# Attention beside a gated feed-forward: queries in bursts of eight heads, values three heads behind the scores, output projection one head later

## The chip, the cores and the metric

The kernel runs on one core of one Trainium2 chip. The metric is the device time of one execution in microseconds (us): the median of three runs before is 560.81 (560.77 to 560.82).

Engine names as the profile has them: PE is TensorE (matmul), PEld its weight loads, DVE is VectorE, ACT is ScalarE, POOL is GpSimd, SP is SyncE. "SPq" or "POOLq" is an engine's queue of instructions, where DMAs are issued. PSUM has eight banks of 512 float32 columns.

## What is computed

The input x has 2048 rows of 448. It is layer-normalized and goes two ways: through attention with 16 query heads of 256 over the last 512 keys and values of a cache (8 key-value heads, each for two query heads), and through a feed-forward of width 1792. The result is x plus the product of both.

```
xn = layernorm(x)
q = xn @ wq                      # 16 heads of 256
p = softmax(q @ k.T / 16)        # the last 512 keys of each of 8 groups
s = (p @ v) @ wo
g = silu((gelu(xn @ w_gate) * (xn @ w_up)) @ w_down)
out = x + s * g
```

## The kernel before

The rows are cut into four chunks of 512 (`NQC`), each chunk into four tiles of 128 (`TPC`). Every operation is recorded with what it reads and writes (`Rec.op`, lines 65 to 96); the order of recording is the order on each engine, and a wait is put in where an operation depends on one of another engine. Each engine works its own list in that order.

**First part (lines 506 to 521).** For each chunk: gate and up projection with two 64-row matmuls side by side (L370), gelu (L374), product (L376), down projection (L382). The down projection of the last chunk is kept back to fill gaps at the start of attention (`fill`, lines 527 to 530).

**Second part (lines 531 to 559), attention.** There are 64 steps i, one for each chunk and head (`NI` = 4 x 16). Within a step, t runs over the four row tiles:

- `scores(i, t)`: two matmuls (L420) into bank 4 or 5 in turn; ScalarE's exponential with row sum (L424) into a buffer `pr`; VectorE's reciprocal (L426) and normalization (L427); a DMA transpose on SP's queue into `pT` (L236). Nine buffers `pr` are used in turn.
- `values(i', e_)`: at t = 0 and 2, four matmuls (L440) for half of an earlier head, and a copy into `oT` (L446 on VectorE, L448 on ScalarE for the last two heads). It is called for the first time at step 10 of scores (4i + t >= 10), so it runs two and a half heads behind. Its bank follows a list of eight that repeats every four heads: `(0, 6, 0, 6, 0, 1, 6, 6)`; at heads with i%4 = 3 both calls use bank 6.
- `outproj(G, t, part)`: at t = 1 and 3, from head 6 on, four matmuls each (L460). One head's two calls finish one row tile t of a group G of four heads; group G takes heads 4G + 6 to 4G + 9. The sum over groups is kept in `acc` by VectorE (L479, L481). After the last group of a chunk (G = 3, 7, 11; in the last chunk after G = 14) GpSimd multiplies by the gate into `tmp[t % 2]` (L485) and adds x (L487), into `ofin` or, in the last chunk, `acc`. When all four tiles are done, POOL's queue sends `ofin` out and loads the next chunk's `xr` (L233).
- `q_burst(G)`: after the first scores and values of heads with i%4 = 3, the queries of the next four heads: 56 matmuls of 64 rows (L406), which run side by side in pairs, into banks 0 to 3, and four evictions by ScalarE (L410), each for two heads, into `qT` (six heads).
- `silu(n)`: after heads 7, 10, 13, ... 52. ScalarE's tanh of half the gate into `tmp[n % 2]` (L499), and two GpSimd operations (L500, L502).

**The end (lines 549 to 559).** After the last scores, five calls of values and two of outproj are left ("vvovovv"), then group 15, in pieces and with the final operations on VectorE (L469, L471) and the output DMAs.

`tmp` is one buffer with two slots. It is used by `silu` and by the finishing of a chunk.

Of the kernel before, what the change touches and what calls it, by code (L numbers as in the profile page):

```python
# [5 lines left out]
ACT = mybir.ActivationFunctionType  # L6
ALU = mybir.AluOpType
BF16 = mybir.dt.bfloat16
# [3 lines left out]
P = 128  # L12
# [129 lines left out]
def bass_recurrent_scan__sliding_block_cached__geglu_ffn__prompt_kernel(nc, A_x, A_k, A_v, A_wq, A_wo, B_x, B_wg, B_wu, B_wd, out):  # L142
    _, S, D = A_x.shape
    Hkv, Sk, Dh = A_k.shape[1], A_k.shape[2], A_k.shape[3]
    HD = A_wq.shape[1]
    Hq = HD // Dh
# [12 lines left out]
    with es:  # L159
        off = [16512]  # L160

        def sb(name, shape, dt, at=None):
            n = 4 if dt == F32 else 2
            for x in shape[1:]:
                n *= x
            if at is None:
                at = off[0]
                off[0] += (n + 31) // 32 * 32
            return R.place(name, shape, dt, at), at + (n + 31) // 32 * 32
# [24 lines left out]
        hb, ffn_end = sb("hb", [P, NHB, QC], BF16)  # L194


        NPT = 4
        qT, at = sb("qT", [P, 6, NE, QC], BF16, gu_at)
        oT = [None, None]
        oT[0], at = sb("oT0", [P, 4 * NE, QC], BF16, at)  # L200
        xr, at = sb("xr", [P, TPC, D], BF16, at)
        assert at <= x_at
        pT, at = sb("pT", [P, NPT, NJ, QC], BF16, x_at)
        pr = []
        while at + 2 * W <= d_at:
            t_, at = sb("pr%d" % len(pr), [P, W], BF16, at)
            pr.append(t_)
        at = hb_at
        while at + 2 * W <= ffn_end:
            t_, at = sb("pr%d" % len(pr), [P, W], BF16, at)  # L210
            pr.append(t_)
        NPR = len(pr)
        oT[1], at = sb("oT1", [P, 4 * NE, QC], BF16, d_at)
        acc, at = sb("acc", [P, TPC, D], F32, at)
        tmp, at = sb("tmp", [P, 2, D], F32, at)
        ofin, at = sb("ofin", [P, TPC, D], BF16, at)
        assert at <= hb_at, (at, hb_at)
        psum = es.enter_context(nc.psum_tensor("ps", [P, 8 * 512], F32))

        def bank(b, n=512):  # L220
            return psum[:, b * 512:b * 512 + n]
# [171 lines left out]
        NI = NQC * Hq  # L393
        NG = NI // 4

        def q_burst(G):

            c, h0 = divmod(4 * G, Hq)
            for n in range(4):
                hp, e_ = divmod(n, 2)  # L400
                s, i = 2 * (n % 2) if G else (4, 0, 2, 0)[n], (4 * G + 2 * hp) % 6

                def run(e, hp=hp, e_=e_, s=s):
                    for k in range(NK):
                        for b, lo in ((s, 0), (s + 1, HP)):
                            ins = e.matmul(bank(b), lhsT=wq[lo:lo + HP, k, h0 // 2 + hp, e_ * P:(e_ + 1) * P],  # L406
                                           rhs=xnT[lo:lo + HP, c, k, :], start=k == 0, stop=k == NK - 1)
                    return ins
                pe(run, r=xn(c) + [("wq", lo, k) for lo in range(2) for k in range(NK)], w=[("ps", s), ("ps", s + 1)])
                act(lambda e, e_=e_, s=s, i=i: e.activation(  # L410
                    qT[:, i:i + 2, e_, :], psum[:, s * 512:(s + 2) * 512].rearrange("p (a q) -> p a q", a=2), ACT.Copy),
                    r=[("ps", s), ("ps", s + 1)], w=[("qT", i, e_), ("qT", i + 1, e_)])

        def scores(i, t):
            g, n = (i % Hq) // 2, i * TPC + t
            b, s = 4 + n % 2, n % NPR

            def run(e):
                for k in range(NE):
                    ins = e.matmul(bank(b), lhsT=qT[:, i % 6, k, t * P:(t + 1) * P], rhs=kT[:, g, k, :],  # L420
                                   start=k == 0, stop=k == NE - 1)
                return ins
            pe(run, r=[("kT", g), ("qT", i % 6, 0), ("qT", i % 6, 1)], w=[("ps", b)])
            act(lambda e: e.activation(pr[s][:, :], bank(b), ACT.Exp, scale=scale, accum_out=den[:, s:s + 1]),  # L424
                r=[("ps", b)], w=[("pr%d" % s,), ("den", s)])
            dve(lambda e: e.reciprocal(rden[:, s:s + 1], den[:, s:s + 1]), r=[("den", s)], w=[("rden", s)])  # L426
            dve(lambda e: e.tensor_scalar(pr[s][:, :], pr[s][:, :], rden[:, s:s + 1], None, op0=ALU.mult),  # L427
                r=[("pr%d" % s,), ("rden", s)], w=[("pr%d" % s,)])
            dmaT(pT[:, i % NPT, :, t * P:(t + 1) * P], pr[s][:, :], r=[("pr%d" % s,)], w=[("pT", i % NPT, t)], lane="p%d" % s)

        def values(i, e_):
            g = (i % Hq) // 2
            idx = (i % 4) * NE + e_
            at = 2 * i + e_ + 5

            b = (0, 6, 0, 6, 0, 1, 6, 6)[at % 8] if at < 2 * NI else (0, 6, 0, 6, 1)[at - 2 * NI]

            def run(e):
                for j in range(NJ):
                    ins = e.matmul(bank(b), lhsT=V[:, j, g, e_ * P:(e_ + 1) * P], rhs=pT[:, i % NPT, j, :],  # L440
                                   start=j == 0, stop=j == NJ - 1)
                return ins
            pe(run, r=[("pT", i % NPT, t) for t in range(TPC)] + [("V", j) for j in range(NJ)], w=[("ps", b)])
            dst, key = oT[(i // 4) % 2][:, idx, :], ("oT%d" % ((i // 4) % 2), idx)
            if i < NI - 2:
                dve(lambda e: e.tensor_copy(dst, bank(b)), r=[("ps", b)], w=[key])  # L446
            else:
                act(lambda e: e.activation(dst, bank(b), ACT.Copy), r=[("ps", b)], w=[key])  # L448

        def outproj(G, t, part, half=None):  # L450

            n8 = 4 * NE
            lo, hi = (0, D) if half is None else (half * D // 2, (half + 1) * D // 2)
            b = ((2, 2), (3, 5), (7, 4), (0, 6))[t][half or 0] if G == NG - 1 else (7, 7, 7, 4)[t] if G == NG - 2 else 7
            c, h0 = divmod(4 * G, Hq)
            end = c == NQC - 1

# [10 lines left out]
            if end and h0 == Hq - 4:  # L468
                dve(lambda e: e.tensor_tensor(tmp[:, t % 2, lo:hi], bank(b, D)[:, lo:hi], gy[:, n, lo:hi], ALU.mult),  # L469
                    r=[("ps", b), ("gy", n)], w=[("tmp", t % 2)])  # L470
                dve(lambda e: e.tensor_tensor(ofin[:, t, lo:hi], tmp[:, t % 2, lo:hi], acc[:, t, lo:hi], ALU.add),  # L471
                    r=[("tmp", t % 2), ("acc", t)], w=[("ofin", t, lo)])
                if t == TPC - 1:
                    dma("sync" if half else "scalar", o_view[:, c, t, lo:hi], ofin[:, t, lo:hi], r=[("ofin", t, lo)])
                elif half != 0:
                    dma("sync", o_view[:, c, t, :], ofin[:, t, :], r=[("ofin", t, 0), ("ofin", t, lo)])
                return
            if h0 == 0:
                dve(lambda e: e.tensor_copy(acc[:, t, :], bank(b, D)), r=[("ps", b)], w=[("acc", t)])  # L479
# [1 line left out]
                dve(lambda e: e.tensor_tensor(acc[:, t, :], bank(b, D), acc[:, t, :], ALU.add),  # L481
                    r=[("ps", b), ("acc", t)], w=[("acc", t)])
            if h0 == Hq - 4 or end and h0 == Hq - 8:
                dst, key = (acc, ("acc", t)) if end else (ofin, ("ofin", t))
                pool(lambda e: e.tensor_tensor(tmp[:, t % 2, :], acc[:, t, :], gy[:, n, :], ALU.mult),  # L485
                     r=[("acc", t), ("gy", n)], w=[("tmp", t % 2)])
                pool(lambda e: e.tensor_tensor(dst[:, t, :], tmp[:, t % 2, :], xr[:, t, :], ALU.add),  # L487
                     r=[("tmp", t % 2), ("xr",)], w=[key])
                if t == TPC - 1 and not end:
                    dma("gpsimd", o_view[:, c, :, :], ofin[:, :, :], r=[("ofin", t) for t in range(TPC)])  # L490
                    load_xr(c + 1)

        def load_xr(c):
            dma("gpsimd", xr[:, :, :], x_view[:, c, :, :], w=[("xr",)])

        def silu(n):

# [23 lines left out]
                    load_piece()  # L521
        assert not pieces
        act(lambda e: e.activation(small[:, 2:3], small[:, 0:1], ACT.Exp), r=[("eps",)], w=[("warm",)])
        q_burst(0)
        load_xr(0)

        fill = {}
# [5 lines left out]
        for i in range(NI):  # L533
            for t in range(TPC):
                scores(i, t)
                if 4 * i + t in fill:
                    down(NQC - 1, *fill[4 * i + t])
                if t % 2 == 0 and 4 * i + t >= 10:
                    values(*pv.pop(0))
                if 6 <= i and t % 2:  # L540
                    outproj(*outs[0], range(2 * t - 2, 2 * t + 2))
                    if t == TPC - 1:
                        outs.pop(0)
                if t == 0 and i % 4 == 3 and i + 1 < NI:
                    q_burst(i // 4 + 1)
            if 7 <= i and (i - 7) % 3 == 0 and (i - 7) // 3 < NT:
                silu((i - 7) // 3)

        for what in "vvovovv":
            if what == "v":  # L550
                values(*pv.pop(0))
            else:
                outproj(*outs.pop(0), range(4 * NE))
# [36 lines left out]
```

## Time and profile before

| what | value |
|---|---|
| median of 3 runs | 560.81 us |
| the profiled execution, whole | 561.18 us |
| its span from first to last instruction | 559.4 us |
| granted TensorE clock | 1.000 |
| VectorE normalization L427, one | 416 ns mean |
| exponential L424, one | 597 ns |
| eviction of a query pair L410, one | 1024 ns |
| transposes of the probabilities, issue to landing | 2.4 us median, 256 of them |

The profile is taken from one execution, whose own time is 0.37 us above the median of the others. Durations come from it. The busy time of TensorE is the sum of stretches in which at least one matmul runs; matmuls are pipelined, so one lasts 379 ns although the next starts much sooner. In the timeline a row gives start, length, engine, line, operation and tiles; "x4" merges four like operations, and a bracket tells how long the engine stood idle before it and who released it.

### The profile page before, as it was taken

Reading aid. Unit: us, or ns where it says so; the run is one execution under the profiler, and the core shown is the slowest. Engines: PE = TensorE matmul, PEld = TensorE weight load, DVE = VectorE, ACT = ScalarE, POOL = GpSimd, SP = SyncE. Lnnn points to the kernel's source line nnn. Section 1 sums busy time; section 2 is a strip of 40 time slices with the busy share of each in tenths; the row PEclk is TensorE's granted clock in tenths of the full one; section 3 lists DMA queues with packets and bytes.
Section 4 is the critical chain, followed back from the end, with each engine's and each line's share of the span. In section 5 each row is a group of like instructions: output and inputs, shape, how many; then the busy total and the mean of one; then the engine's idle time right before and its main releaser. Section 6 shows DMA issues by size and latency. Waiting matters only on the chain.

```text
span 559.4 us, 9865 instructions
## 1 busy us (share of the span) xinstructions
PE 549.0 (98%) x3499; PEld 257.2 (46%) x3532; DVE 322.9 (58%) x835; ACT 296.1 (53%) x673; POOL 90.1 (16%) x125
## 2 busy tenths in 40 slices
PE   7999999999999999999999999999999999999997
PEld 3544444444444444444444444444444444444445
DVE  5636446143464847474846657484747484755674
ACT  4324233247655565556565656656565656565641
POOL 0232323200000111013501101232100021400023
PEclk9999999999999999999999999999999999999999
DMA  8994746972453435353664344445535353645352
GB/s 193 276 191 86 138 102 136 247 137 65 94 85 68 97 64 99 69 91 64 143 98 94 73 86 71 81 84 137 101 67 99 63 95 71 147 79 101 70 92 52
DMA packets 169552, 58.83 MB, mean 105 GB/s; under 512 B 160160, under 2 KB 166432, under 8 KB 169504
## 3 DMA queue, kind: packets, MB, share of 16 engines
q1 hardware_dynamic: 166208, 45.50, 44.2%
q0 software_dynamic: 3152, 12.65, 8.9%
q8 instruction: 28, 0.46, 0.4%
q14 instruction: 20, 0.16, 0.1%
q10 hardware_dynamic: 144, 0.06, 0.0%
HBM read 17.92 MB, written 1.84 MB: 35 GB/s over the span
## 4 chain that ended last, share of the span: by engine, by line
PE 95%; DMA 1%; DVE 1%; issue 1%; SPq 1%; ACT 0%
PE ps L440 20%; PE ps L420 19%; PE ps L406 18%; PE ps L460 16%; PE ps L370 15%; PE ps L382 8%; DMA wgu<-in_B_w_up_dram 1%; SPq L233 1%; DVE tmp L469 0%; DVE ofin L471 0%; DVE pr L427 0%; DVE oT L446 0%; DVE rden L426 0%; ACT pr L424 0%
## 5 line engine op out<-in xcount | busy, mean ns | idle before, releaser
L424 ACT ACTIVATE pr<-ps 128x512 bf16<-128x512 f32 x256 | 152.8, 597 | 116.6 <-PE ps L420 112.5
L420 PE MATMUL ps<-kT,qT 128*128 128x512 bf16 x481 | 145.4, 379 | 3.3 <-issue 2.5
L440 PE MATMUL ps<-pT,V 128*128 128x512 bf16 x510 | 130.8, 379 | 0.6 <-DVE rden L426 0.4
L426 DVE RECIPROCAL rden<-den 128x1 f32<-128x1 f32 x256 | 41.5, 162 | 152.4 <-ACT pr L424 134.3
L460 PE MATMUL ps<-wo,oT 128*128 128x448 bf16 (+1 forms) x536 | 116.3, 344 | 0.0
L427 DVE TENSOR_SCALAR pr<-pr,rden 128x512 bf16<-128x512 bf16 x256 | 106.4, 416 | 9.0
L406 PE MATMUL ps<-xnT,wq 64*128 64x512 bf16 x896 | 99.5, 376 | 0.0
L410 ACT ACTIVATE qT<-ps 128x1024 bf16<-128x1024 f32 x64 | 65.5, 1024 | 49.8 <-PE ps L406 49.8
L370 PE MATMUL ps<-xnT,wgu 64*128 64x512 bf16 x784 | 85.5, 376 | 1.0 <-ACT xnT L322 0.8
L446 DVE CAST oT<-ps 128x512 bf16<-128x512 f32 x124 | 84.6, 682 | 0.6 <-PE ps L440 0.5
L440 PEld LDWEIGHTS ps<-pT,V 128*128 128x128 bf16 x512 | 49.9, 98 | 60.8 <-issue 1.2
L460 PEld LDWEIGHTS ps<-wo,oT 128*128 128x128 bf16 x536 | 52.3, 98 | 51.1
L420 PEld LDWEIGHTS ps<-kT,qT 128*128 128x128 bf16 x512 | 48.5, 98 | 57.1 <-issue 7.3
L376 DVE TENSOR_TENSOR actT<-ps,hb 128x512 bf16<-128x512 f32 x56 | 38.1, 685 | 57.5 <-ACT hb L374 55.7
L406 PEld LDWEIGHTS ps<-xnT,wq 64*128 64x128 bf16 x896 | 42.4, 94 | 55.9 <-DVE acc L481 4.2
L374 ACT ACTIVATE hb<-ps 128x512 bf16<-128x512 f32 x56 | 33.4, 597 | 51.8 <-PE ps L370 51.8
L370 PEld LDWEIGHTS ps<-xnT,wgu 64*128 64x128 bf16 x784 | 39.2, 94 | 46.5 <-issue 2.5
L424 ACT ACTIVATION_READ_ACCUMULATOR pr<-ps 128x1 f32 x256 | 49.9, 195 | 0.0
L500 POOL TENSOR_SCALAR tmp<-tmp 128x448 f32<-128x448 f32 x16 | 9.1, 572 | 233.9 <-ACT tmp L499 233.9
L382 PE MATMUL ps<-wd,actT 128*128 128x448 bf16 x224 | 46.2, 353 | 0.1
L485 POOL TENSOR_TENSOR tmp<-acc,gy 128x448 f32<-128x448 f32 x16 | 16.6, 1035 | 123.2 <-DVE acc L481 123.2
L382 PEld LDWEIGHTS ps<-wd,actT 128*128 128x128 bf16 x224 | 21.7, 98 | 22.2 <-issue 1.3
(43 smaller groups left out, 171.7 us busy)
## 6 DMA issues: line engine op xcount, KB each, us to landing
pT<-pr SPq DMA_TRANSPOSE x256, 2.4
wq<-in_A_wq_dram POOLq DMA_DIRECT2D x14, 256.0 KB, 4.3
wo<-in_A_wo_dram POOLq DMA_DIRECT2D x4, 896.0 KB, 10.1
V<-in_A_v_cache_dram POOLq DMA_DIRECT2D x4, 512.0 KB, 5.8
xr<-in_A_x_dram POOLq DMA_DIRECT2D x4, 448.0 KB, 4.8
wd<-in_B_w_down_dram SPq DMA_DIRECT2D x1, 1568.0 KB, 17.6
wgu<-in_B_w_gate_dram SPq DMA_DIRECT2D x3, 448.0 KB, 10.3
wgu<-in_B_w_up_dram SPq DMA_DIRECT2D x3, 448.0 KB, 11.8
```

What stands on the lines that cost most here:

```text
L370: ins = e.matmul(bank(b), lhsT=wgu[lo:lo + HP, k, f * P:(f + 1) * P], rhs=xnT[lo:lo + HP, c, k, :], start=k == 0, stop=k == NK - 1)
L376: dve(lambda e: e.tensor_tensor(actT[:, f, :], bank(s + 1), hb[:, n % NHB, :], ALU.mult), r=[("ps", s + 1), ("hb", n % NHB)], w=[("actT", f)])
L382: pe(lambda e, f=f: e.matmul(bank(b, D), lhsT=actT[:, f, t * P:(t + 1) * P], rhs=wd[:, f, :], start=f == 0, stop=f == NF - 1), r=[("actT", ...
L406: ins = e.matmul(bank(b), lhsT=wq[lo:lo + HP, k, h0 // 2 + hp, e_ * P:(e_ + 1) * P], rhs=xnT[lo:lo + HP, c, k, :], start=k == 0, stop=k == ...
L410: act(lambda e, e_=e_, s=s, i=i: e.activation(qT[:, i:i + 2, e_, :], psum[:, s * 512:(s + 2) * 512].rearrange("p (a q) -> p a q", a=2), AC ...
L420: ins = e.matmul(bank(b), lhsT=qT[:, i % 6, k, t * P:(t + 1) * P], rhs=kT[:, g, k, :], start=k == 0, stop=k == NE - 1)
L424: act(lambda e: e.activation(pr[s][:, :], bank(b), ACT.Exp, scale=scale, accum_out=den[:, s:s + 1]), r=[("ps", b)], w=[("pr%d" % s,), ("de ...
L426: dve(lambda e: e.reciprocal(rden[:, s:s + 1], den[:, s:s + 1]), r=[("den", s)], w=[("rden", s)])
L427: dve(lambda e: e.tensor_scalar(pr[s][:, :], pr[s][:, :], rden[:, s:s + 1], None, op0=ALU.mult), r=[("pr%d" % s,), ("rden", s)], w=[("pr%d ...
L440: ins = e.matmul(bank(b), lhsT=V[:, j, g, e_ * P:(e_ + 1) * P], rhs=pT[:, i % NPT, j, :], start=j == 0, stop=j == NJ - 1)
L446: dve(lambda e: e.tensor_copy(dst, bank(b)), r=[("ps", b)], w=[key])
L460: ins = e.matmul(bank(b, D)[:, lo:hi], lhsT=oT[G % 2][:, idx, t * P:(t + 1) * P], rhs=wo[:, h0 * NE + idx, lo:hi], start=idx == 0, stop=id ...
```

## The change

1. Query bursts: the first two make four heads (before head 0 and in head 3), then in heads 7, 15, 23, ... 55 eight heads each. `qT` becomes five buffers of two heads each.
2. Values run three heads behind the scores (first at step 12).
3. The output projection starts at head 7, so group G takes heads 4G + 7 to 4G + 10. The silus stay where they are.
4. After the last scores six calls of values and three of outproj are left ("vvovovovv").
5. `ofin` is gone: x and result share `xr`, so its reload waits for the output's DMA. The buffers `pr` are ten.

```diff
-        qT, at = sb("qT", [P, 6, NE, QC], BF16, gu_at)
+        for n in range(3):
+            qT[n], at = sb("qT%d" % n, [P, 2, NE, QC], BF16, at)
...
-        def q_burst(G):
+        def q_slot(i):
+            p = i // 2
+            p = p if p < 3 else (p - 3) % NQP
+            return qT[p], "qT%d" % p, i % 2
+        def q_burst(i0, heads):
...
-            at = 2 * i + e_ + 5
-            b = (0, 6, 0, 6, 0, 1, 6, 6)[at % 8] if at < 2 * NI else (0, 6, 0, 6, 1)[at - 2 * NI]
+            at = 2 * i + e_ + 6
+            b = (0, 6, 0, 6, 0, 1, 6, 6)[at % 8] if at < 2 * NI else (0, 6, 1, 0, 6, 1)[at - 2 * NI]
...
-            b = ((2, 2), (3, 5), (7, 4), (0, 6))[t][half or 0] if G == NG - 1 else (7, 7, 7, 4)[t] if G == NG - 2 else 7
+            b = ((2, 2), (3, 5), (4, 7), (0, 6))[t][half or 0] if G == NG - 1 else (7, 7, 4, 7)[t] if G == NG - 2 else 7
...
-                dst, key = (acc, ("acc", t)) if end else (ofin, ("ofin", t))
+                dst, key = (acc, ("acc", t)) if end else (xr, ("xr", t))
...
-                    dma("gpsimd", o_view[:, c, :, :], ofin[:, :, :], r=[("ofin", t) for t in range(TPC)])
+                    dma("gpsimd", o_view[:, c, :, :], xr[:, :, :], r=[("xr", t) for t in range(TPC)])
                     load_xr(c + 1)
...
-        q_burst(0)
+        q_burst(0, 4)
...
-                if t % 2 == 0 and 4 * i + t >= 10:
+                if t % 2 == 0 and 4 * i + t >= 12:
                     values(*pv.pop(0))
-                if 6 <= i and t % 2:
+                if 7 <= i and t % 2:
                     outproj(*outs[0], range(2 * t - 2, 2 * t + 2))
...
-                if t == 0 and i % 4 == 3 and i + 1 < NI:
-                    q_burst(i // 4 + 1)
+                if t == 0 and (i == 3 or i % 8 == 7) and i + 1 < NI:
+                    q_burst(i + 1, 4 if i == 3 else 8)
             if 7 <= i and (i - 7) % 3 == 0 and (i - 7) // 3 < NT:
                 silu((i - 7) // 3)

-        for what in "vvovovv":
+        for what in "vvovovovv":
```

More of the change, by code (lines that the diff above doesn't have):

```diff
@@ L194, in bass_recurrent_scan__sliding_block_cached__geglu_ffn__prompt_kernel, with fill_pr @@
         hb, ffn_end = sb("hb", [P, NHB, QC], BF16)
-        NPT = 4
-        qT, at = sb("qT", [P, 6, NE, QC], BF16, gu_at)
+        NPT, NQP = 4, 5
+        qT = [None] * NQP
         oT = [None, None]
+        at = gu_at
+        for n in range(3):
+            qT[n], at = sb("qT%d" % n, [P, 2, NE, QC], BF16, at)
         oT[0], at = sb("oT0", [P, 4 * NE, QC], BF16, at)
         xr, at = sb("xr", [P, TPC, D], BF16, at)
-        assert at <= x_at
-        pT, at = sb("pT", [P, NPT, NJ, QC], BF16, x_at)
[L204 to L212, printed above, removed]
+        pr = []
+        def fill_pr(at, end):
+            while at + 2 * W <= end:
+                t_, at = sb("pr%d" % len(pr), [P, W], BF16, at)
+                pr.append(t_)
+        fill_pr(at, x_at)
+        pT, at = sb("pT", [P, NPT, NJ, QC], BF16, x_at)
+        fill_pr(at, d_at)
         oT[1], at = sb("oT1", [P, 4 * NE, QC], BF16, d_at)
@@ L215, in bass_recurrent_scan__sliding_block_cached__geglu_ffn__prompt_kernel @@
         tmp, at = sb("tmp", [P, 2, D], F32, at)
-        ofin, at = sb("ofin", [P, TPC, D], BF16, at)
-        assert at <= hb_at, (at, hb_at)
+        for n in range(3, NQP):
+            qT[n], at = sb("qT%d" % n, [P, 2, NE, QC], BF16, at)
+        assert at >= hb_at, (at, hb_at)
+        fill_pr(at, nc.sbuf_usable_end)
+        NPR = len(pr)
         psum = es.enter_context(nc.psum_tensor("ps", [P, 8 * 512], F32))
@@ L394, in bass_recurrent_scan__sliding_block_cached__geglu_ffn__prompt_kernel @@
         NG = NI // 4
-        def q_burst(G):
-            c, h0 = divmod(4 * G, Hq)
-            for n in range(4):
+        def q_slot(i):
[3 more added lines that the diff above has]
+        def q_burst(i0, heads):
+            c, h0 = divmod(i0, Hq)
+            for n in range(heads):
                 hp, e_ = divmod(n, 2)
-                s, i = 2 * (n % 2) if G else (4, 0, 2, 0)[n], (4 * G + 2 * hp) % 6
+                s = 2 * (n % 2) if i0 else (4, 0, 2, 0)[n]
+                buf, name, _ = q_slot(i0 + 2 * hp)
                 def run(e, hp=hp, e_=e_, s=s):
@@ L409, in q_burst @@
                 pe(run, r=xn(c) + [("wq", lo, k) for lo in range(2) for k in range(NK)], w=[("ps", s), ("ps", s + 1)])
-                act(lambda e, e_=e_, s=s, i=i: e.activation(
-                    qT[:, i:i + 2, e_, :], psum[:, s * 512:(s + 2) * 512].rearrange("p (a q) -> p a q", a=2), ACT.Copy),
-                    r=[("ps", s), ("ps", s + 1)], w=[("qT", i, e_), ("qT", i + 1, e_)])
+                act(lambda e, e_=e_, s=s, buf=buf: e.activation(
+                    buf[:, :, e_, :], psum[:, s * 512:(s + 2) * 512].rearrange("p (a q) -> p a q", a=2), ACT.Copy),
+                    r=[("ps", s), ("ps", s + 1)], w=[(name, e_)])
         def scores(i, t):
@@ L416, in scores @@
             b, s = 4 + n % 2, n % NPR
+            buf, name, a = q_slot(i)
             def run(e):
                 for k in range(NE):
-                    ins = e.matmul(bank(b), lhsT=qT[:, i % 6, k, t * P:(t + 1) * P], rhs=kT[:, g, k, :],
+                    ins = e.matmul(bank(b), lhsT=buf[:, a, k, t * P:(t + 1) * P], rhs=kT[:, g, k, :],
                                    start=k == 0, stop=k == NE - 1)
                 return ins
-            pe(run, r=[("kT", g), ("qT", i % 6, 0), ("qT", i % 6, 1)], w=[("ps", b)])
+            pe(run, r=[("kT", g), (name, 0), (name, 1)], w=[("ps", b)])
             act(lambda e: e.activation(pr[s][:, :], bank(b), ACT.Exp, scale=scale, accum_out=den[:, s:s + 1]),
@@ L470, in outproj @@
                     r=[("ps", b), ("gy", n)], w=[("tmp", t % 2)])
-                dve(lambda e: e.tensor_tensor(ofin[:, t, lo:hi], tmp[:, t % 2, lo:hi], acc[:, t, lo:hi], ALU.add),
-                    r=[("tmp", t % 2), ("acc", t)], w=[("ofin", t, lo)])
+                dve(lambda e: e.tensor_tensor(xr[:, t, lo:hi], tmp[:, t % 2, lo:hi], acc[:, t, lo:hi], ALU.add),
+                    r=[("tmp", t % 2), ("acc", t)], w=[("xr", t, lo), ("xr", t)])
                 if t == TPC - 1:
-                    dma("sync" if half else "scalar", o_view[:, c, t, lo:hi], ofin[:, t, lo:hi], r=[("ofin", t, lo)])
+                    dma("sync" if half else "scalar", o_view[:, c, t, lo:hi], xr[:, t, lo:hi], r=[("xr", t, lo)])
                 elif half != 0:
-                    dma("sync", o_view[:, c, t, :], ofin[:, t, :], r=[("ofin", t, 0), ("ofin", t, lo)])
+                    dma("sync", o_view[:, c, t, :], xr[:, t, :], r=[("xr", t, 0), ("xr", t, lo)])
                 return
@@ L487, in outproj @@
                 pool(lambda e: e.tensor_tensor(dst[:, t, :], tmp[:, t % 2, :], xr[:, t, :], ALU.add),
-                     r=[("tmp", t % 2), ("xr",)], w=[key])
+                     r=[("tmp", t % 2), ("xr", t)], w=[key])
                 if t == TPC - 1 and not end:
-                    dma("gpsimd", o_view[:, c, :, :], ofin[:, :, :], r=[("ofin", t) for t in range(TPC)])
+                    dma("gpsimd", o_view[:, c, :, :], xr[:, :, :], r=[("xr", t) for t in range(TPC)])
                     load_xr(c + 1)
         def load_xr(c):
-            dma("gpsimd", xr[:, :, :], x_view[:, c, :, :], w=[("xr",)])
+            dma("gpsimd", xr[:, :, :], x_view[:, c, :, :], w=[("xr", t) for t in range(TPC)])
         def silu(n):
```

## The prediction

> **What bounds the kernel now.** I read the page's engine table and its chain first, then the waits of TensorE, then the timeline around a query burst, around the chunk's last output projection, and at the end.
>
> ```profile
> PE 549.0 (98%) x3499; PEld 257.2 (46%) x3532; DVE 322.9 (58%) x835; ACT 296.1 (53%) x673; POOL 90.1 (16%) x125
> ...
> PE 95%; DMA 1%; DVE 1%; issue 1%; SPq 1%; ACT 0%
> ```
>
> TensorE carries 95% of the chain that ended last. The waits of TensorE alone (us in total, times, longest) show how little is left to win from waiting:
>
> ```profile
> PE ps L420 <- issue: 2.5, 16, 0.2
> ...
> PE ps L440 <- DVE rden L426: 0.4, 1, 0.4
> ```
>
> The 16 "issue" waits are the 16 query bursts. So whatever makes TensorE wait is added to the time almost one for one, and the only thing to save is at the edges of bursts. One burst, from the timeline:
>
> ```profile
> 250.12 1.03 PE L440 MATMUL ps<-pT,V 128*128 128x512 bf16 x4
> ...
> 251.07 5.73 PEld L406 LDWEIGHTS ps<-xnT,wq 64*128 64x128 bf16 x56 [0.42 <-DVE acc L481]
> 251.08 6.22 PE L406 MATMUL ps<-xnT,wq 64*128 64x512 bf16 x56
> ...
> 257.22 0.11 PEld L420 LDWEIGHTS ps<-kT,qT 128*128 128x128 bf16 x2 [0.42 <-issue]
> ...
> 257.67 0.92 PE L460 MATMUL ps<-wo,oT 128*128 128x448 bf16 x4
> ```
>
> Starts of consecutive 512-column matmuls lie 0.216 us apart in the trace, of 448-column ones 0.189. Four values matmuls take 4 x 0.216 = 0.86, but the burst starts 0.96 after them: 0.10 at its entry. Its 28 pairs (the two 64-row halves run side by side) and the two scores matmuls behind them should take 30 x 0.216 = 6.48; the output projection starts 6.59 after the burst: 0.11 at its exit. A burst costs 0.21 beside its matmuls, whatever its length.
>
> **The change part by part.**
>
> *Bursts of eight.* The bursts fall from 16 to 9 (four heads, four heads, seven times eight); the matmuls stay. Gain 7 x 0.21 = 1.4 us. Inside a burst ScalarE evicts a pair of banks in 1.02 us (L410), while TensorE fills one in 28/4 x 0.216 = 1.51, so a longer burst builds no queue there. The five pair buffers and ten probability buffers (nine before) are free when they are written again.
>
> *The longer stretch between bursts.* SP issues one transpose per 1.31 us (starts of sixteen in a row, 181.23 to 200.96); outside bursts a head takes 4 x (0.43 + 0.43 + 0.38) = 4.97, 1.24 per transpose. The queue falls behind by 0.27 us per head: 1.1 us in four heads, 2.2 in eight. From a scores matmul to its transpose's issue it is 2.2 us (133.05 to 135.20), to landing 2.4 more, together 6.8 with that backlog. Values three heads behind read the last quarter of a head nine score steps, 9 x 1.24 = 11.2 us, after it was started. Covered, at nothing; if contention doubled the landing and each of seven stretches ended late, about 1 us each.
>
> *The end.* Two small holds of before, both visible as weight loads that come late, are
>
> ```profile
> 540.27 0.56 PEld L440 LDWEIGHTS ps<-pT,V 128*128 128x128 bf16 x4 [0.65 <-issue]
> ...
> 548.25 1.42 PEld L440 LDWEIGHTS ps<-pT,V 128*128 128x128 bf16 x8 [0.57 <-issue]
> ```
>
> The first cost 0.34 us (interval of loads less the matmuls' own): two values in a row use bank 6, and VectorE's copy out of the first (L446) was late behind a normalization that took 0.96 instead of 0.35 while GpSimd ran. In the changed kernel that GpSimd work starts after the last head's scores. The second, 0.32, waited for the last transpose; now one more output projection (8 x 0.189 = 1.5 us) lies ahead of those values, more than the extra 1.1 us of backlog. Gain 0.7. The moved output projections and values themselves are the same matmuls in other places: nothing.
>
> *Bank 6 twice, without a burst between.* At every fourth head (i%4 = 3) two values in a row use bank 6. A burst lay between them in 15 of 16 cases; now it does only in half. Without GpSimd in the way the copy ends in time: at X+3.26 in the clock used below, load wanted at X+3.46. In heads 11 and 35, though, the silu's GpSimd work comes just there, as it did at 538 us. Cost 2 x 0.34 = 0.7; ends 0 and 1.
>
> *The output projection a head later: the step that decides.* The silus stay after heads 7, 10, 13 and so on, and both they and the finishing of a chunk (L485, L487) use the two-slot buffer tmp. Silu n uses slot n%2, row t of the projection slot t%2. For G = 3, 7, 11 the rows were finished in heads 18-21, 34-37, 50-53; now in 19-22, 35-38, 51-54. Before, where a silu followed a head that finished a row, the slots differed: head 19 (silu 4 with row 1), 34 (9 with row 0), 37 (10 with row 3), 52 (15 with row 2). Now they are the same at all four such heads: 19 (4 with row 0), 22 (5 with row 3), 37 (10 with row 2), 52 (15 with row 1). ScalarE's tanh (L499) must then wait until GpSimd has read the slot in L487, and all exponentials of the next head stand behind the tanh in ScalarE's order. Before, in head 19, where the slots differed:
>
> ```profile
> 260.15 0.92 PE L460 MATMUL ps<-wo,oT 128*128 128x448 bf16 x4
> ...
> 260.91 0.59 PE L420 MATMUL ps<-kT,qT 128*128 128x512 bf16 x2
> 260.94 0.57 ACT L499 ACTIVATE tmp<-gy 128x448 f32<-128x448 bf16 x1
> ...
> 261.54 0.60 ACT L424 ACTIVATE pr<-ps 128x512 bf16<-128x512 f32 x1
> 261.54 0.62 DVE L481 TENSOR_TENSOR acc<-ps,acc 128x448 f32<-128x448 f32 x1
> ...
> 262.24 1.04 POOL L485 TENSOR_TENSOR tmp<-acc,gy 128x448 f32<-128x448 f32 x1 [9.03 <-DVE acc L481]
> ...
> 263.36 1.03 POOL L487 TENSOR_TENSOR ofin<-tmp,xr 128x448 bf16<-128x448 f32 x1
> 263.39 0.59 PE L420 MATMUL ps<-kT,qT 128*128 128x512 bf16 x2
> ```
>
> With X = 260.15, the start of the last projection matmuls: tanh at X+0.79, the next head's first exponential at X+1.39, its third scores (which needs that exponential's bank; there are two) at X+3.24. GpSimd's read ends at X+4.24. If tanh waits for it: tanh at about X+4.3, exponential 0.60 later at X+4.9, ended X+5.5, scores about 0.2 later at X+5.7 instead of X+3.24. **TensorE loses 2.45 us.** After head 22 a burst follows at X+2.15: its third piece (X+2.15+3.02 = X+5.17) needs the first eviction, which follows the exponential by one pace of 0.71: X+5.6, ended X+6.65, piece at X+6.85. Loss 1.65. Sum 3 x 2.45 + 1.65 = 9.0 us. Before shows no wait of ScalarE for GpSimd, so the hand-over is bounded by neighbours: nothing at all, or the 0.36 that the load's matmul at 540 came behind its copy (540.16 to 540.52). That gives 8.2 to 10.5; I take the middle. Below that only if ScalarE did not wait in order.
>
> [...] ScalarE's rows here are all in program order, but before has no blocked one to show it. [...]
>
> *xr in place of ofin.* The reload of xr now waits on GpSimd for the output's landing (4.3 us) and the silu behind it waits too; its result is needed many heads later, the next tanh comes three heads later: nothing, and if that cover went, another 2 us.
>
> **Sum.** -1.4 - 0.7 + 0.7 + 9.0 = +7.6. Against the profiled execution's own 561.18 (span 559.40 and 1.78 around it) that is 568.8; the median of the runs is 0.37 lower, so 568.4.
>
> **Rivals.**
> - *ScalarE is not held* (or the GpSimd read is done in time): then only the edges count, -1.4 - 0.7 + 0.7 = -1.4, about 559.4, faster. For it: tanh never waited before. Against: slots and order, from the code. It decides if tanh starts before about X+1.9 (X+0.79 plus the 1.05 us by which the exponential was early).
> - *Held, but half as long*, because GpSimd or VectorE comes sooner: about 4.5 us less, 564. Against: L481, L485, L487 keep the same distances in every such head (X+1.39, 2.09, 3.21).
> - *The clock drops after each hold.* Row: the granted clock reads 1.00 throughout, also after the 1.09 us pause at 5.38, yet TensorE's first seven or so matmuls ran at 0.427 apart instead of 0.216. If each of four holds cost eight such steps, 4 x 8 x 0.21 = 6.8: 575. [...]
> - *The values catch the late transposes:* seven stretches at up to 1 us on top: 570 to 575.
>
> **How the numbers follow.** Held as worked out 0.74 (566 to 571); half held 0.08; clock 0.06; transposes 0.06; not held 0.06. The main case's bounds: 8.2 - 2.5 = +5.7 and 10.5 - 1.1 + 1 = +10.4, from 566.5 to 571.2; I take 565.5 to 571.5, which leaves out about 0.2. A difference of 0.2% is about what can be told from no change here: faster 0.06, same 0.02, slower 0.92.
>
> **What would show it.** Right: four waits of tanh for GpSimd's second operation, each about 3.5 us; TensorE idle 2.4 us in heads 20, 38, 53 and 1.6 in the burst after head 22; nine exits; no late load at the end. Wrong: tanh with no wait, or idle TensorE ahead of values (L453) instead of scores, or matmuls more than 0.216 apart after a hold.

## The result, and the profile after

The changed kernel takes 570.75 us (median of five, 570.70 to 572.62), the kernel before 560.81 (560.49 to 561.08, five): 1.0175 times as long, 95% interval 1.0162 to 1.0189. The profiled execution took 572.62 us with a span of 570.8, 11.4 more than the span of before. Forecast were 568.4 us, and +7.6 for the profiled execution.

From the page of the changed kernel, the engine table, the row of the granted clock in 40 slices, and the chain by engine:

```profile
PE 553.6 (97%) x3498; PEld 259.4 (45%) x3532; DVE 320.6 (56%) x835; ACT 295.8 (52%) x673; POOL 89.9 (16%) x125
...
PEclk9999999999999999998999999999999999899999
...
PE 88%; issue 4%; DVE 3%; POOL 2%; ACT 2%; SPq 1%; DMA 1%; ACTq 0%; POOLq 0%
```

The same matmuls keep TensorE busy 4.6 us longer, the granted clock dips in two slices where it was 9 throughout (a third dip, at 383 to 386 us, lies across two slices of 14 us and shows in neither), and TensorE's share of the chain fell from 95% to 88%: GpSimd and ScalarE are on it now. The waits of the changed kernel (us in total, times, longest) name the cause:

```profile
ACT tmp L512 <- POOL xr L500: 13.5, 4, 3.4
...
PE ps L433 <- ACT pr L437: 6.2, 3, 2.1
...
PE ps L433 <- issue: 1.4, 9, 0.2
...
PE ps L418 <- ACT qT L422: 1.0, 1, 1.0
...
PE ps L453 <- DMA pT<-pr: 0.3, 1, 0.3
```

Four tanhs (L512) wait for GpSimd's second operation, 3.4 us each, a wait that before did not have. Three times scores then wait for an exponential, and once a burst for an eviction. The burst exits are nine instead of sixteen. Around the first of the four, the timeline of the changed kernel:

```profile
258.60 0.62 DVE L494 TENSOR_TENSOR acc<-ps,acc 128x448 f32<-128x448 f32 x1
...
259.30 1.03 POOL L498 TENSOR_TENSOR tmp<-acc,gy 128x448 f32<-128x448 f32 x1 [13.86 <-DVE acc L494]
...
259.70 0.92 PE L473 MATMUL ps<-wo,oT 128*128 128x448 bf16 x4
260.41 1.03 POOL L500 TENSOR_TENSOR xr<-tmp,xr 128x448 bf16<-128x448 f32 x1
261.48 0.58 ACT L512 ACTIVATE tmp<-gy 128x448 f32<-128x448 bf16 x1 [3.37 <-POOL xr L500]
261.96 0.58 ACT L437 ACTIVATE pr<-ps 128x512 bf16<-128x512 f32 x1
...
262.68 0.60 PE L433 MATMUL ps<-kT,qT 128*128 128x512 bf16 x2 [2.06 <-ACT pr L437]
```

The tanh starts 0.04 us after L500's end, the exponential 0.48 after the tanh's start, the scores 0.14 after the exponential's end. The four output projections of 259.70 end their stream at 259.70 + 4 x 0.189 = 260.46, so TensorE loses 262.68 - 260.46 = **2.22 us**; the bracket says 2.06 because it counts the last projection as busy to its own end, 259.70 + 0.92 = 260.62. In the burst after head 22 it is 1.22:

```profile
278.19 3.20 PE L418 MATMUL ps<-xnT,wq 64*128 64x512 bf16 x28
...
280.30 0.58 ACT L512 ACTIVATE tmp<-gy 128x448 f32<-128x448 bf16 x1 [3.38 <-POOL xr L500]
...
282.43 9.24 PE L418 MATMUL ps<-xnT,wq 64*128 64x512 bf16 x84 [1.04 <-ACT qT L422]
```

These 28 matmuls are two pieces of the burst. They run in pairs, so they take 28 x 0.108 = 3.02 us; the third piece was due at 281.21 and came at 282.43.

What follows the hold of 262.68 is seen best in a table of stretches (columns: stretch, its length, then busy time and instructions of TensorE, its weight loads, VectorE, ScalarE and GpSimd, then the granted clock, DMA share, GB/s):

```profile
262.00:263.00 1.00, 0.32 (x2) 0.20 (x3) 0.30 (x2) 1.00 (x4) 0.78 (x2) 1.00 0.45 82
...
264.00:265.00 1.00, 1.00 (x4) 0.43 (x3) 0.96 (x4) 0.01 (x1) 0.00 (x0) 0.50 0.00 0
265.00:266.00 1.00, 1.00 (x4) 0.30 (x2) 0.96 (x4) 0.50 (x2) 0.00 (x0) 0.50 0.65 131
...
267.00:268.00 1.00, 1.00 (x6) 0.45 (x5) 0.62 (x1) 0.51 (x2) 0.30 (x1) 1.00 0.25 49
```

Four matmuls are counted in a microsecond, against six at 267 us: the granted clock is 0.50, for 3.41 us from 263.55 by the trace's clock record. The intervals between weight loads in it are 1.69 us longer in sum than the same loads' intervals at full clock. I call such a stretch a half-clock window. The same follows the holds at 382 (half clock from 383.02) and 485 us (from 485.42).

**The account of the profiled execution** against that of before, in us: holds 3 x 2.22 + 1.22 = 7.9; half clock 3 x 1.69 = 5.1; two bank-6 holds of 0.26 at 204 and 365 us, +0.5; the end 0.46 of hold instead of 0.66, -0.2; burst edges 7 x 0.21, -1.5; and the same point in the first scores came 0.4 earlier (137.87 against 138.26). Sum +11.4, measured 11.4. The other four executions lie 1.9 us lower. Only the profiled one has a trace, but the mean granted clock of each is on record: 0.991 in the profiled one, 0.994 in three, 0.997 in one. A half-clock window takes 3.41 x 0.5 / 570 = 0.003 off the mean (a fall after the last matmul can take another 0.001, as in e1), so that is three of them, two and one, and the 1.9 us are about one. The execution with one should be faster by another 1.7 us and took 570.78; what it lost instead is open.

### The profile page after: what moved, and what is told of

Same layout as the page of the kernel before. It is cut to its first block, busy times and chain, and to the rows that moved or that the text cites. A ratio compares the mean times of both kernels' runs of the same rounds, so it can differ in the third digit from the quotient of the medians.

```text
span 570.8 us, 9858 instructions
## 1 busy us (share of the span) xinstructions
PE 553.6 (97%) x3498; PEld 259.4 (45%) x3532; DVE 320.6 (56%) x835; ACT 295.8 (52%) x673; POOL 89.9 (16%) x125
## 3 DMA queue, kind: packets, MB, share of 16 engines
HBM read 17.92 MB, written 1.84 MB: 35 GB/s over the span
## 4 chain that ended last, share of the span: by engine, by line
PE 88%; issue 4%; DVE 3%; POOL 2%; ACT 2%; SPq 1%; DMA 1%; ACTq 0%; POOLq 0%
PE ps L433 18%; PE ps L453 17%; PE ps L418 17%; PE ps L375 15%; PE ps L473 14%; PE ps L387 8%; ACT pr L437 1%; SPq L241 1%; POOL tmp L498 1%; POOL xr L500 1%; DVE pr L440 1%; DVE tmp L482 0%; DMA pT<-pr 0%; DVE xr L484 0%; DVE stats L293 0%
## 5 line engine op out<-in xcount | busy, mean ns | idle before, releaser
L433 PE MATMUL ps<-kT,qT 128*128 128x512 bf16 x493 | 149.6, 383 | 8.2 <-ACT pr L437 6.2
L473 PE MATMUL ps<-wo,oT 128*128 128x448 bf16 (+1 forms) x536 | 118.0, 348 | 0.0
L440 DVE TENSOR_SCALAR pr<-pr,rden 128x512 bf16<-128x512 bf16 x256 | 103.9, 406 | 9.0
L418 PE MATMUL ps<-xnT,wq 64*128 64x512 bf16 x896 | 98.4, 376 | 1.0 <-ACT qT L422 1.0
L418 PEld LDWEIGHTS ps<-xnT,wq 64*128 64x128 bf16 x896 | 42.9, 94 | 55.9 <-DVE acc L494 2.1
L498 POOL TENSOR_TENSOR tmp<-acc,gy 128x448 f32<-128x448 f32 x16 | 16.5, 1034 | 108.0 <-DVE acc L494 108.0
```

Source lines behind the costliest of these rows:

```text
L433: ins = e.matmul(bank(b), lhsT=buf[:, a, k, t * P:(t + 1) * P], rhs=kT[:, g, k, :], start=k == 0, stop=k == NE - 1)
L473: ins = e.matmul(bank(b, D)[:, lo:hi], lhsT=oT[G % 2][:, idx, t * P:(t + 1) * P], rhs=wo[:, h0 * NE + idx, lo:hi], start=idx == 0, stop=id ...
```

## The experiments

The theory after the result: the change costs time because the silu's tanh and the finishing of a chunk now meet in one slot of `tmp`, at four heads; the holds of TensorE are paid once as idle time and, where the clock falls, again. The rivals: the longer bursts, the later transposes, or the output projections moved to the end cost it by themselves. e1 to e4 were measured beside one set of runs of the kernel before (median 561.28 of 29), e5 to e7 beside another (561.11 of 17).

### e1: the changed kernel, silu in the other slot

```diff
-            s = n % 2
+            s = (n + 1) % 2
```

> The changed kernel, with one character of the silu changed: it uses the other slot of tmp, (n + 1) % 2. Theory (the tanh held by GpSimd's read of its slot): no tanh waits for GpSimd, the clock never falls to one half, and what is left is 7 burst edges saved at 0.21 us (-1.4), two bank-6 holds of 0.27 (+0.5) and the end (0.46 of hold instead of 0.66): about 559.7 us, from 559.0 to 560.5. Rival (longer bursts, late transposes or the shared xr make the kernel slow): within 1 us of 570.75.

Measured: 559.45 us (559.24 to 560.73), 0.9967 times the kernel before, interval 0.9951 to 0.9984. Head 19 again, from its timeline:

```profile
257.32 0.92 PE L473 MATMUL ps<-wo,oT 128*128 128x448 bf16 x4
...
258.11 0.57 ACT L512 ACTIVATE tmp<-gy 128x448 f32<-128x448 bf16 x1
...
260.56 0.59 PE L433 MATMUL ps<-kT,qT 128*128 128x512 bf16 x2
```

The tanh starts 0.79 after the projection with no bracket, and the third scores 3.24 after it, to the hundredth as before. No tanh waits for GpSimd, and the clock stays up until the last matmul. One slot index takes away the 11 us: the theory holds, and the change without the collision is faster than before. I call this kernel the mended one. Its last values did not wait at all in the profiled execution; no slow transpose fell into its last stretch (see below).

### e2: the kernel before, silu in the other slot

The same edit of the kernel before. Nothing else changes: bursts of four, old lags.

> The kernel before, with the silu's slot turned over, (n + 1) % 2; bursts, lags and buffers are as they were. Theory: tanh meets the slot of the row that its head finished in heads 19, 34, 37 and 52; three holds of 2.23 us (scores of heads 20, 38, 53) and one of 1.2 in the burst of head 35, 7.9 in all, and for each hold that falls wholly into one clock window 1.7 more: 568.7 to 573.8, most likely about 570.4. Rival (the slot is no matter, the bursts or the lags are): 560.8.

Measured: 572.27 us (570.75 to 573.82), 1.0186 times before, interval 1.0154 to 1.0218. Its waits:

```profile
ACT tmp L499 <- POOL ofin L487: 13.5, 4, 3.4
...
PE ps L420 <- ACT pr L424: 6.6, 3, 2.5
```

The same four waits of 13.5 us in all appear, with none of the change in the kernel, and the time rises by as much. So the collision is enough by itself. Of its three holds in scores the clock fell after two (384.58 and 486.98 us), not after the first, which ended at 265.46. Over its six executions the time goes with the mean granted clock: 570.75 and 570.91 us at 0.996, 572.19 and 572.35 at 0.994, 572.88 at 0.993, 573.82 at 0.991.

### e3: bursts of eight alone, all lags as before

```diff
-            at = 2 * i + e_ + 6
+            at = 2 * i + e_ + 5
...
-                if t % 2 == 0 and 4 * i + t >= 12:
+                if t % 2 == 0 and 4 * i + t >= 10:
...
-                if 7 <= i and t % 2:
+                if 6 <= i and t % 2:
```

(and the end's order and banks as before).

> Bursts of eight alone, with all lags as before (values from step 10, projection from head 6, the old end), xr in place of ofin. Theory: slots differ again without touching the silu, so no holds; the burst edges give -1.4, one bank-6 hold at a silu in head 11 and one in head 35 +0.5, and the end is as before or waits up to 1 us more because the transposes are 1.1 us further behind: 559.4 to 561. Rival (late transposes are what the longer lag is for): values wait at the end of each of seven long stretches, 1 us or more each, over 566.

Measured: 562.92 us (561.89 to 564.59), 1.0028 times before, interval 1.001 to 1.0046. Slower than the theory's range. No tanh waits; two other things do, both at work in the timeline of its end:

```profile
539.86 1.02 PE L453 MATMUL ps<-pT,V 128*128 128x512 bf16 x4 [0.18 <-DVE rden L439]
...
543.69 1.02 PE L453 MATMUL ps<-pT,V 128*128 128x512 bf16 x4 [0.76 <-DMA pT<-pr]
...
550.08 1.89 PE L453 MATMUL ps<-pT,V 128*128 128x512 bf16 x8 [1.47 <-DMA pT<-pr]
```

The first is a bank-6 hold. With the old lag GpSimd's finishing (L498) meets the two values in a row at heads 19, 35, 51 and 63, and a silu at 11: five holds of 0.34, 1.7 us, and not two. The others are values that wait for transposes: 0.92 and 1.63 us by the intervals of the weight loads, 2.6 in all, and not up to 1. With -1.5 at the edges, the 0.66 of before's end counted off, and first scores that came 0.3 earlier, this makes +1.8, as the span shows (561.2 against 559.4); the medians differ by +1.6. The rival was wrong about the seven stretches, which show no such wait, but right at the end: after eight heads without a burst the old order of the end is too short. One slow transpose (2.36 us, at 544.9) lies in that end, so a part of the 1.63 is its doing; how much, one trace does not tell. The longer lag belongs to the longer bursts.

### e4: the longer lags alone

```diff
-                if t == 0 and (i == 3 or i % 8 == 7) and i + 1 < NI:
-                    q_burst(i + 1, 4 if i == 3 else 8)
+                if t == 0 and i % 4 == 3 and i + 1 < NI:
+                    q_burst(i + 1, 4)
```

(and the silu in the other slot).

> The longer lags alone: bursts of four heads as before, values three heads behind, projection a head later, and the silu in the other slot so that nothing is held. Theory: the lags are worth the end's holds alone, -0.2 to -0.7: 560.1 to 560.7. Rival (the lags themselves cost time, by the projections moved to the end): 562 or more.

Measured: 560.44 us (560.18 to 564.11), 0.9987, interval 0.9968 to 1.0006: the interval does not exclude that the two are equal, and the direction is the one that was expected. e1 differs from it by the bursts alone and is 1.0 us faster. e1 has two bank-6 holds (0.5) that e4 does not have, and e4 an output projection that comes 0.2 late (286.45), so seven burst edges are worth 1.0 + 0.5 - 0.2 = 1.3 us, against 7 x 0.21 = 1.5 worked out.

### e5: the mended kernel with one collision

```diff
-            s = (n + 1) % 2
+            s = n % 2 if n == 10 else (n + 1) % 2
```

> The mended kernel (silu in the other slot) with one conflict put back: silu 10 alone uses the slot of the row that head 37 finished. Theory: one wait of tanh of 3.4 us, TensorE idle 2.23 us in head 38, so 559.45 + 2.2 = 561.7 where the clock stays, and 1.7 more, 563.4, in executions in which the idle time lies wholly in one 3.41 us window of the clock; the times should fall into these two groups. Rival (the cost of the holds is the clock's fall, the idle time is absorbed): 559.5 or 561.2.

Measured: 561.81 us median of twelve; 1.0022 times before, interval 1.001 to 1.0034. The twelve times fall into two groups: six from 561.44 to 561.53, one at 562.10, five from 563.25 to 564.18. The lower group is 2.0 us over e1, the upper 1.9 higher still (by medians). The mean granted clock is 0.997 in each of the five, which is one half-clock window, and 1.000 in each of the seven others. The profiled execution is one of the upper group; its stretches around the hold:

```profile
376.00:377.00 1.00, 0.00 (x0) 0.00 (x0) 0.00 (x0) 0.20 (x1) 0.77 (x1) 1.00 0.32 64
...
380.00:381.00 1.00, 1.00 (x4) 0.38 (x3) 0.96 (x4) 0.00 (x0) 0.00 (x0) 0.50 0.34 67
...
383.00:384.00 1.00, 1.00 (x7) 0.31 (x7) 0.44 (x3) 0.51 (x2) 0.91 (x1) 1.00 0.64 130
```

TensorE does nothing at 376, runs at one half at 380 and at full clock again at 383. One collision costs its idle time in every execution and a half-clock window in five of these twelve. The rival, that the idle time is absorbed, is out.

### e6: the product with the gate on VectorE

The changed kernel with its collisions, but L498 on VectorE:

```diff
-                pool(lambda e: e.tensor_tensor(tmp[:, t % 2, :], acc[:, t, :], gy[:, n, :], ALU.mult),
+                dve(lambda e: e.tensor_tensor(tmp[:, t % 2, :], acc[:, t, :], gy[:, n, :], ALU.mult),
```

> The changed kernel with its conflicts, but the product with the gate (L498) done by VectorE instead of GpSimd. Theory: the slot comes free about 0.5 us sooner, so the three holds are about 1.75 us and the burst's 0.75; 7.9 - 1.9 = 6.0 us of idle. If the clock falls as before: 568.9; if a shorter idle time keeps the clock up: 565.5. Rival (time is lost by GpSimd's work as such, or by VectorE's load): no faster than 570.7.

Measured: 566.91 us (566.77 to 568.62, four runs), 1.0109, interval 1.0094 to 1.0124. From the timeline at head 37:

```profile
377.14 0.62 DVE L498 TENSOR_TENSOR tmp<-acc,gy 128x448 f32<-128x448 f32 x1
...
377.84 1.03 POOL L500 TENSOR_TENSOR xr<-tmp,xr 128x448 bf16<-128x448 f32 x1 [4.00 <-DVE tmp L498]
...
378.96 0.58 ACT L512 ACTIVATE tmp<-gy 128x448 f32<-128x448 bf16 x1 [3.10 <-POOL xr L500]
...
380.17 0.60 PE L433 MATMUL ps<-kT,qT 128*128 128x512 bf16 x2 [1.79 <-ACT pr L437]
```

The three holds of the scores are 1.84, 1.96 and 1.90 us, 0.3 shorter and not 0.5; the one in the burst is 1.3 as before, and not 0.75. The time lies between the two that were forecast. The clock does not fall after any of the holds here, and the mean granted clock is 1.000 in all four executions (also in the one of 568.62, whose extra 1.7 us are something else, without a trace). So the chain through the slot sets the hold, as the theory has it, and 0.9 us less idle time saved 3.8 us of the median. The rest is the clock: with the two half-clock windows of most executions of the changed kernel (0.994) at 1.69 each it comes to 4.3, and two output projections that came 0.24 late here, behind VectorE's sum L494 (at 266.8 and 485.6), take 0.5 back.

### e7: the mended kernel, one value of the pair in bank 1

```diff
-            b = (0, 6, 0, 6, 0, 1, 6, 6)[at % 8] if at < 2 * NI
+            b = (0, 6, 0, 6, 0, 1, 6, 6, 0, 6, 0, 6, 0, 1, 6, 1)[(at + 8) % 16] if at < 2 * NI
```

> The mended kernel (silu in the other slot), and the second of the two values at heads 3, 11, 19, ... 59 in bank 1 instead of bank 6. Theory: the two bank-6 holds of 0.26 us in heads 11 and 35 go: 559.45 - 0.5 = 558.9, no wait of TensorE for VectorE left after the first scores. Rival (another wait takes their place): 559.4.

Measured: 559.17 us (558.72 to 560.73, five runs), 0.9962 times before, interval 0.9949 to 0.9974. The two bank-6 holds are gone from the weight loads and no other took their place in attention (the profiled execution, the slowest of the five, lost 1.7 us in the first part to a late DMA of `xnT`). In time it is 0.3 us less than e1, which the intervals of the two cannot tell from nothing. It has the lowest median of those tried, 0.4% below the kernel before.

## Why the prediction was right, and where its sizes were off

**The step that decides** (the output projection a head later) was right in every place: the four heads, the four waits (forecast 3.5 us each, measured 3.4), scores held in heads 20, 38 and 53, and the burst after head 22. Its size was a little off: 2.22 and 1.22 instead of 2.45 and 1.65, 7.9 instead of 9.0 in all. With X as in the prediction, the start of head 19's last projection matmuls (257.22 here), L500 ended at X+4.22, forecast X+4.24; after it the tanh followed in 0.04, the exponential came 0.48 behind the tanh instead of 0.60, and the scores 0.14 behind its end instead of 0.2. The 0.60 had been read from a row in which the exponential had its own scores to wait for (they ended at 261.50, it started at 261.54). That an exponential does not pass a held tanh, on which the 9.0 rest, was the author's estimate from the order of the code, and no row of before shows it; in the changed kernel the exponential behind the tanh of 261.48 had its scores at 257.98 + 0.59 = 258.57 and started at 261.96.

**The clock was the step that failed.** The prediction had it as a rival, with 0.06, beside the main case, whose sum has it at nothing: the author's estimate, which no run shows. The holds happened and the clock fell after them, in the profiled execution after all three of 2.22 us. It cost 1.69 each, what the rival had named for each (6.8 for four). One of the prediction's own signs of being wrong, matmuls more than 0.216 apart after a hold, came true with it (starts 0.427 apart at 263.98). The rows of before did not show that so short a hold is enough: from the first projections to its last matmul, its longest pause of TensorE was 0.4 us. Here 2.22 us were enough, three times of three in this execution.

**The number was right partly by luck.** Without the clock the holds, at 7.9 and not 9.0, and the smaller terms would have made some 567 us. With two half-clock windows, as the mean clock of most executions has them, 3.4 us came on top, and 570.75 lies inside the stated range. The room at its upper end had been left for slower hand-overs and late transposes, which did not use it; the execution with three of them, 572.62, lies above it. In the bounds themselves the gains listed add to 2.1 and not 2.5, so the lower one should read 566.9; nothing hung on that.

**Bursts:** seven edges at 0.21, right (1.3 by e1 and e4); 7 x 0.21 is 1.5, and the sum had 1.4. **Evictions in a long burst:** no queue built up, right: in e1 no query matmul (L418) waits for an eviction.

**The longer stretch:** covered, right, but with less room than was said: in the profiled execution the last values waited 0.46 us for the last transpose. Some 13 to 18 of the 256 transposes take 1.5 to 2.5 us on SP's queue instead of 1.2, at places that differ in part from run to run. One of them, at 554.6 and of 2.40 us, came in the last stretch; in e1 none did after 485.6, and no value waited. So the end's gain was 0.2 here and 0.7 in e1. e3 shows what the older lag would have cost.

**Bank 6:** the two heads were right, the size 0.26 instead of 0.34.

**xr in place of ofin:** nothing, right: GpSimd waited 8.2 us for the output's landings, and no one waited for it.

**The rivals:** "not held" is what e1 does (forecast 559.4, measured 559.45); "held half as long" did not happen; the late transposes of the seven stretches did not happen either, they cost time only at the end, in the profiled execution (0.46) and in e3.

## What to carry to other kernels

When a step is moved by a fixed amount, look at every buffer that it shares with a step that is not moved, and write down the slots at each meeting: a parity that kept two users apart can put them together at every meeting, and a tuned schedule hides that it rests on it. ScalarE kept the order of the code here: the exponential of 261.96, whose scores had ended 3.39 us earlier, stood behind a tanh of 0.58. So a wait of a side job is a wait of all that is queued behind it, and the side job's buffer matters although its own work is small. And when TensorE is held for about 2 us, count the clock as a second price, and count it as a chance: one hold of 2.2 us brought the clock down in five of twelve executions of e5, and those of 1.84 to 1.96 in e6 did not.

## What the runs showed of the hardware that was not expected

The half-clock stretches are 3.41 us long and lie on a grid: they begin at 263.55, 383.02 and 485.42 us in the changed kernel, 119.47 and 102.40 apart, which is 35.0 and 30.0 times 3.413. The clock's first rise, at 4.14, where the starts of matmuls go from 0.427 to 0.216 us apart, is on the same grid (76.0 steps before 263.55). A window, below, is one step of this grid. The grid does not start with the kernel: the first rise came at 4.14 us here, at 5.70 in e2, 6.63 in e5 and 6.13 in e6. That would explain the two groups of e5, if the clock falls by how much of the idle time lies in one window, which is the author's reading of the holds below. A hold of 2.22 us put at random on a grid of 3.41 lies wholly in one window in (3.41 - 2.22) / 3.41 = 35% of cases, an estimate; in e5 it was five of twelve. Taking the windows of each execution from its grid, the six holds after which the clock fell (three in the changed kernel, two in e2, one in e5) had between 2.18 and 2.23 us of idle time in the window that ended where the half clock began. The first hold of e2 ran from 263.23 to 265.46, over a window's end at 265.11, with 1.88 in the first window and 0.35 in the next, and the clock stayed. In e6 the three holds had 1.62, 1.96 and 1.30 us in one window, and in the bursts it was 1.2 to 1.3, and the clock stayed. After the last matmul it fell at the end of a window with 2.26 us of idle time in e1, and not with 1.76 in e2, which fits. So, by this reading, the bound lies between 1.96 and 2.18 us of idle time in a window of 3.41, an estimate, as far as these few holds tell; none was made to fall in between, and the grid of e6, whose clock never fell while matmuls ran, is reckoned from its first rise.
